# Attention and routed expert: a third buffer for transposed squares, no square or low part asked for at a chunk's last slot but one, and the last 64 keys' squares on ScalarE

## The chip, the cores and the metric

The kernel runs on one core of one Trainium2 chip. The metric is the time of one execution on the device, in microseconds. Three runs of the kernel before gave 2127.13, 2130.31 and 2130.52 us; the median is 2130.31 us.

## The reference

Eight batches go through squared-ReLU attention whose queries and keys are the same matrix `z`, then through an expert that works on the 128 best tokens of each batch. Cut to what matters:

```python
# B, S, D, d_qk = 8, 3136, 256, 64;  F = 1024;  capacity = 128
scores = (1 / S) * z @ z.transpose(0, 2, 1)          # symmetric
x = u * (np.maximum(scores, 0) ** 2 @ v)
out = x.copy()
for b in range(B):
    s = x[b] @ w_gate
    top = the 128 tokens with the largest s
    y = np.maximum(x[b, top] @ w1, 0) @ w2
    out[b, top] = x[b, top] + sigmoid(s[top])[:, None] * y
```

## The kernel before, in words

**Chunks and slots.** The 3136 queries of a batch are cut into seven chunks: c0 to c4 of 512 queries, c5 of 256 and c6 of 320. For each chunk the program goes through the keys in 13 slots, s0 to s12: twelve take a pair of key blocks (2 x 128 keys), and the last, the single slot, takes the 64 keys that are left. There are 8 x 7 x 13 = 728 slots in one sequence. In each, TensorE adds squares times `V` into four PSUM banks of the chunk (`acc`, L641; the pool has five banks). A square is split into a high part `hi` and a low part `lo` = square - hi, and both are multiplied. The products with `hi` come first, so `lo` may be ready a little later. At the end of a chunk the single slot is multiplied by `Vr` in place of `V`.

**New and old slots.** The scores are symmetric. A slot whose scores have not yet been worked out in this batch is new. TensorE multiplies them (`sc`, L510; for the single slot L494), ScalarE takes the ReLU (`a`, L514; single L500) and writes the square's high part (`hi`, L524; single L501). Then `a` is squared in place: for a pair by ScalarE (L530) or by VectorE (L534), as running sums of planned costs decide, and for the single slot by VectorE (L503). The low part is a subtraction, `lo`, on GpSimd or VectorE (both L614), as the same sums decide, and for the single slot on VectorE (L551). Squares that a later chunk needs are also transposed by VectorE into a staging tile `aT` (L577, L595 for the chunk's own block, L557 for the single slot), which SyncE stores to memory (L583, L589, L597, L565). An old slot fetches such squares back as `qk`, copies the high part (L474) and takes its low part. The tag `aT` has two buffers, so a transpose into it waits until the store of the tile two before has landed.

**What sets the order.** The program writes each engine's instructions out in an order of its own, slot by slot. In a slot, scores for three slots later are begun (`more_scores`), the products are issued (`mix`), and then a list of closing calls (`posts`) is run. Normally `settle_scores` stands in the middle of that list. It issues the outstanding squares, transposes and low parts of the slots ahead, which the function `low` writes, with the transpose ahead of the `lo`. `square_scores` issues the outstanding squares alone.

**A chunk's end.** At the single slot `finish` reads the four banks: ScalarE scales two of them (L722), and VectorE adds and multiplies, twice L735 and L736. Only then are banks free for the next chunk. In the slot before, s11, the list of closing calls is split. One call is made at once: `square_scores` in chunks c0 to c5 (not in the very first chunk), `settle_scores` otherwise. The rest is held for s12, where it comes behind L735 and L736. The code at L1653 is:

```python
if k + 2 < len(slots) and len(slots[k + 1][2]) == 1:

    now = square_scores if c <= WHOLE and (b or c) else settle_scores
    posts, held_posts = [now], [fn for fn in posts if fn is not settle_scores]
```

Between these calls the router's steps stand: gates and their sums (L943 to L967), the merge of the best tokens of the last batch's late chunks (L1201 to L1267) and the expert's products.

Of the kernel before, what the change touches and what calls it, by code (L numbers as in the profile page):

```python
# [88 lines left out]
def attention_then_routed_ffn(ctx: ExitStack, tc: tile.TileContext, zt, ut, v, wg, w1, w2, cst, cst16, keys, outs, at, cap):  # L89
# [388 lines left out]
    def scores(k):  # L478
# [9 lines left out]
        if n == 1:  # L488
# [12 lines left out]
            nc.scalar.activation(hi[:, 0, :w], a, AF.Square)  # L501
            spend(act=0.39 + 0.0024 * w)
            lows.append((k, a, hi[:, :, :w], (), lambda: nc.vector.tensor_tensor(a, a, a, op=ALU.mult)))  # L503
            return
# [37 lines left out]
    def low(k, a, hi, pieces, square):  # L542
# [5 lines left out]
        if n == 1:  # L548
            w = w // 2
            hi, lo = hi[:, 0], hi[:, 1]  # L550
            nc.vector.tensor_tensor(lo, a, hi.bitcast(F32), op=ALU.subtract)  # L551
            spend(dve=0.25 + 0.002 * w)

        def turned_single():
            x = w // 2
            t = work.tile([P, GT, 2, P], F32, name="aT", tag="aT", bufs=2).rearrange("p m q x -> p (m q x)")[:, :w]
            nc.vector.transpose(  # L557
# [9 lines left out]
        def turned():  # L567
# [3 lines left out]
            elif turns(k):  # L571
                t = work.tile([P, GT, 2, P], F32, name="aT", tag="aT", bufs=2)
                x = w // GT
# [17 lines left out]
            elif is_first(k):  # L591
                t = work.tile([P, GT, 2, P], F32, name="aT", tag="aT", bufs=2).rearrange("p m q x -> p (m q x)")[:, :CH]
                for q in range(2):
                    to = t.rearrange("p (m t q a) -> p q m t a", m=GT, t=2, q=2)[:, q]
                    nc.vector.transpose(to, a[:, q].rearrange("p (m t a) -> p m t a", t=GT, a=Q)[:, :, 2:])  # L595
                    spend(dve=0.08 + 0.0006 * w)
                stores.append(lambda: nc.sync.dma_start(own[b % 2][c].rearrange("p m x -> p (m x)"), t))  # L597
# [681 lines left out]
    def expert(b, st, n, r0=0):  # L1279
# [51 lines left out]
        def turned():  # L1331
            view = st["ps"][:, : NK * P].rearrange("p (k r) -> p k r", r=P)[:, :, :m]
            if merged(b):
                x = work.tile([P, 2, NK, P], F32R, name="xs", tag="aT", bufs=2)
            elif put_off(b) and b == B - 2:
# [262 lines left out]
    for k, (b, c, js, is_old) in enumerate(slots):  # L1598
# [45 lines left out]
        settle_turns()  # L1644
        if len(js) == 1 and c == WHOLE:
            low(*lows.pop(0))
        settle_stores()
# [5 lines left out]
        if k + 2 < len(slots) and len(slots[k + 1][2]) == 1:  # L1653

            now = square_scores if c <= WHOLE and (b or c) else settle_scores
            posts, held_posts = [now], [fn for fn in posts if fn is not settle_scores]
        if late and c >= NCH - late:
# [81 lines left out]
```

## Time and profile before

| what | value |
|---|---|
| median of three runs | 2130.31 us |
| the profiled execution | 2133.84 us, of which the span from first to last instruction is 2132.1 us |
| TensorE busy (PE) | 2037.6 us, 96% of the span |
| VectorE (DVE), ScalarE (ACT), GpSimd (POOL) busy | 72%, 69%, 62% |
| mean granted clock of TensorE | 0.985 of full speed |

TensorE (PE) is the engine to read first. PEld is its weight load, which runs beside the products. SPq is SyncE's queue of DMA issues. In a row of a timeline the first number is the start in us from the start of the span, the second the duration in us; a bracket at the end tells how long the engine had been idle and what ended that.

### The profile page before, as it was taken

To read this page: it belongs to the slowest core of one execution; us is meant where nothing else is said; L and a number is where in the kernel's file an instruction comes from. 1 tells how busy PE (TensorE), PEld (TensorE's weight loads), DVE (VectorE), ACT (ScalarE), POOL (GpSimd) and SP (SyncE) were. 2 spreads that over 40 slices of the span, in tenths; PEclk is the share of its full clock that TensorE was granted. 3 is DMA by queue.
4 is the path that set the end of the run, shared out by engine and by line. 5 is a ranking of instruction groups with operands and counts; after the bars stand their busy time and mean duration, and the time that the engine had idled before them with its cause. 6 is when DMAs were issued, how large, how long until landed. Compare 5 with 4: busy or idle time off the path is not lost.

```text
span 2132.1 us, 51160 instructions
## 1 busy us (share of the span) xinstructions
PE 2037.6 (96%) x19700; PEld 1756.1 (82%) x19700; DVE 1536.0 (72%) x2707; ACT 1462.7 (69%) x1965; POOL 1315.4 (62%) x718
## 2 busy tenths in 40 slices
PE   8999999999899999999989999899998999999997
PEld 5788978879688797888978889788887988778786
DVE  9766688756886568865788568875687766867665
ACT  7676687666776567865778657776587766777553
POOL 5765577735776367763678546775377654776452
PEclk9999999999999999999999999999999999999999
DMA  6788767896668966788657876678866777666842
GB/s 181 199 231 219 223 184 199 243 242 191 186 183 226 249 181 183 211 226 229 191 173 214 233 217 196 186 205 227 229 193 187 195 187 204 192 177 178 225 143 76
DMA packets 450868, 426.94 MB, mean 200 GB/s; under 512 B 136576, under 2 KB 377792, under 8 KB 447808
## 3 DMA queue, kind: packets, MB, share of 16 engines
q1 hardware_dynamic: 449488, 421.18, 70.0%
q8 instruction: 154, 2.52, 0.5%
q0 software_dynamic: 768, 2.10, 0.3%
q14 instruction: 90, 0.74, 0.1%
q10 hardware_dynamic: 368, 0.39, 0.1%
HBM read 248.94 MB, written 174.60 MB: 199 GB/s over the span
## 4 chain that ended last, share of the span: by engine, by line
PE 68%; DMA 7%; DVE 5%; ACT 4%; SPq 3%; issue 2%; POOL 1%; POOLq 0%; ACTq 0%; DVEq 0%
PE acc L641 58%; PE sc L510 7%; DMA qk<-squares 2%; DMA zst<-in_zt 2%; ACT a L514 1%; ACT hi L524 1%; DVE lo L614 1%; PE h L1358 1%; DMA squares_narrow<-aT 1%; DMA squares<-aT 1%; DVE a L534 1%; DVE aT L577 1%; PE y L1401 1%; DVE acc L735 1%; SPq L589 1%
## 5 line engine op out<-in xcount | busy, mean ns | idle before, releaser
L641 PE MATMUL acc<-hi,V 64*128 64x512 f32 (+2 forms) x10752 | 1270.5, 364 | 22.9 <-DVE ut L736 20.6
L641 PEld LDWEIGHTS acc<-hi,V 64*128 64x128 f32 x10752 | 1004.3, 186 | 158.6 <-issue 30.2
L614 POOL TENSOR_TENSOR lo<-a,hi 128x1024 fp32r<-128x1024 f32 (+1 forms) x280 | 634.2, 2267 | 462.0 <-ACT a L530 207.5
L641 PE MATMUL acc<-lo,V 64*128 64x512 f32 (+2 forms) x5376 | 716.4, 364 | 40.4 <-DVE lo L614 26.0
L641 PEld LDWEIGHTS acc<-lo,V 64*128 64x128 f32 x5376 | 520.1, 186 | 106.8 <-DVE lo L614 29.4
L514 ACT ACTIVATE a<-sc 128x1024 f32<-128x1024 f32 (+2 forms) x345 | 327.7, 950 | 268.7 <-PE sc L510 255.3
L577 DVE STREAM_TRANSPOSE aT<-a 128x512 f32<-128x512 f32 (+1 forms) x494 | 317.2, 681 | 213.9 <-ACT a L530 173.9
L474 ACT CAST hi<-qk 128x1024 fp32r<-128x1024 f32 (+2 forms) x327 | 278.9, 855 | 150.8 <-PE acc L641 110.8
L524 ACT ACTIVATE hi<-a 128x1024 fp32r<-128x1024 f32 (+2 forms) x345 | 339.8, 985 | 39.1 <-PE acc L641 17.9
L614 DVE TENSOR_TENSOR lo<-qk,hi 128x1024 fp32r<-128x1024 f32 (+2 forms) x215 | 298.5, 1399 | 60.5 <-ACT hi L474 47.2
L614 POOL TENSOR_TENSOR lo<-qk,hi 128x1024 fp32r<-128x1024 f32 (+2 forms) x112 | 220.8, 1979 | 137.9 <-ACT hi L474 122.1
L530 ACT ACTIVATE a<-a 128x1024 f32<-128x1024 f32 (+2 forms) x261 | 256.4, 982 | 7.5
L534 DVE TENSOR_TENSOR a<-a 128x1024 f32<-128x1024 f32 (+1 forms) x84 | 153.4, 1827 | 63.2 <-ACT hi L524 56.3
L126 POOL TENSOR_TENSOR V<-vst,V 128x512 fp32r<-128x512 f32 x92 | 161.5, 1764 | 17.8 <-ACT V L125 17.2
L754 POOL TENSOR_TENSOR ut<-x,w_run 128x1024 f32<-128x1024 f32 (+2 forms) x52 | 131.5, 2529 | 37.1 <-DVE x L745 36.8
L126 POOL TENSOR_TENSOR ZL<-zst,ZH 64x256 fp32r<-64x256 f32 x70 | 75.8, 1083 | 62.6 <-ACT ZH L125 53.4
L510 PE MATMUL sc<-Z,ZH 64*128 64x512 f32 x480 | 101.6, 390 | 10.1 <-ACT a L514 9.5
L614 DVE TENSOR_TENSOR lo<-a,hi 128x1024 fp32r<-128x1024 f32 (+2 forms) x65 | 83.8, 1289 | 24.4 <-ACT a L530 22.0
L510 PE MATMUL sc<-Z,ZL 64*128 64x512 f32 x480 | 99.5, 378 | 0.8 <-DVE ZL L126 0.8
L510 PE MATMUL sc<-Zl,ZH 64*128 64x512 f32 x480 | 98.7, 378 | 0.0
L735 DVE SCALAR_TENSOR_TENSOR acc<-acc,x 128x512 f32<-128x512 f32 (+2 forms) x112 | 70.0, 625 | 26.4 <-PE acc L641 26.2
L722 ACT ACTIVATE x<-acc 128x512 f32<-128x512 f32 (+2 forms) x112 | 54.5, 538 | 45.4 <-PE acc L641 44.5
(221 smaller groups left out, 1796.9 us busy)
## 6 DMA issues: line engine op xcount, KB each, us to landing
squares<-aT SPq DMA_DIRECT2D x160, 512.0 KB, 3.3
qk<-squares SPq DMA_DIRECT2D x320, 256.0 KB, 6.2
squares_narrow<-aT SPq DMA_DIRECT2D x320, 128.0 KB, 3.2
qk<-squares_narrow SPq DMA_DIRECT2D x80, 512.0 KB, 4.3
out<-x SPq DMA_DIRECT2D x162, 128.0 KB, 3.4
ut<-in_ut SPq DMA_DIRECT2D x40, 512.0 KB, 5.6
vst<-in_v SPq DMA_DIRECT2D x158, 128.0 KB, 2.9
zmv<-in_zt SPq DMA_DIRECT2D x78, 128.0 KB, 4.3
```

Of the source, the lines that this page charges most:

```text
L126: (lo_on or nc.vector.tensor_tensor)(lo, src, hi.bitcast(F32), op=ALU.subtract)
L474: nc.scalar.copy(by(hi), src)
L510: nc.tensor.matmul(ps[:, q, :w], stationary(high, js[0] // 2, q), mov[m][rows], start=i == 0, stop=i == 2)
L514: nc.scalar.activation(a, ps[:, :, :w], AF.Relu)
L524: nc.scalar.activation(pieces[0][0](hi), pieces[0][1], AF.Square)
L530: nc.scalar.activation(a, a, AF.Square)
L534: square = lambda: nc.vector.tensor_tensor(a, a, a, op=ALU.mult)
L577: nc.vector.transpose(to, a[:, q].rearrange("p (m t a) -> p m t a", m=GT, a=Q))
L614: on.tensor_tensor(view(lo), src, view(hi).bitcast(F32), op=ALU.subtract)
L641: nc.tensor.matmul(bank[g][h][:, cols[g]], V[b, j][rows, i, h], mov[rows], start=(b, c, g, h) not in opened, stop=len(js) == 1 and n == 2,)
L735: nc.vector.scalar_tensor_tensor(rest, rest, SCALE * SCALE, sums[h], op0=ALU.mult, op1=ALU.add)
L754: nc.gpsimd.tensor_tensor(wx, runs, consts["wg_run"].rearrange("p (o r) -> p o r", o=1).broadcast_to([P, NB, RUN]), op=ALU.mult,)
```

## The change

There are three edits. The tag `aT` gets three buffers. At s11 the list `posts` is emptied: no square and no low part is asked for there, and all is held for s12. The single slot's in-place square goes from VectorE (L503) to ScalarE (new line 502), right behind the `hi` square, and two planned costs are adjusted to it. For the chunk c5 the outstanding square is called before `low` at the end of its single slot, since it has not been asked for earlier.

```diff
             nc.scalar.activation(hi[:, 0, :w], a, AF.Square)
-            spend(act=0.39 + 0.0024 * w)
-            lows.append((k, a, hi[:, :, :w], (), lambda: nc.vector.tensor_tensor(a, a, a, op=ALU.mult)))
+            nc.scalar.activation(a, a, AF.Square)
+            spend(act=0.52 + 0.0032 * w)
+            lows.append((k, a, hi[:, :, :w], (), lambda: None))
             return
...
             nc.vector.tensor_tensor(lo, a, hi.bitcast(F32), op=ALU.subtract)
-            spend(dve=0.25 + 0.002 * w)
+            spend(dve=0.15 + 0.001 * w)
...
-            t = work.tile([P, GT, 2, P], F32, name="aT", tag="aT", bufs=2).rearrange("p m q x -> p (m q x)")[:, :w]
+            t = work.tile([P, GT, 2, P], F32, name="aT", tag="aT", bufs=3).rearrange("p m q x -> p (m q x)")[:, :w]
...
-                t = work.tile([P, GT, 2, P], F32, name="aT", tag="aT", bufs=2)
+                t = work.tile([P, GT, 2, P], F32, name="aT", tag="aT", bufs=3)
...
-                t = work.tile([P, GT, 2, P], F32, name="aT", tag="aT", bufs=2).rearrange("p m q x -> p (m q x)")[:, :CH]
+                t = work.tile([P, GT, 2, P], F32, name="aT", tag="aT", bufs=3).rearrange("p m q x -> p (m q x)")[:, :CH]
...
-                x = work.tile([P, 2, NK, P], F32R, name="xs", tag="aT", bufs=2)
+                x = work.tile([P, 2, NK, P], F32R, name="xs", tag="aT", bufs=3)
...
         if len(js) == 1 and c == WHOLE:
+            lows[0][-1]()
             low(*lows.pop(0))
...
         if k + 2 < len(slots) and len(slots[k + 1][2]) == 1:
 
-            now = square_scores if c <= WHOLE and (b or c) else settle_scores
-            posts, held_posts = [now], [fn for fn in posts if fn is not settle_scores]
+            posts, held_posts = [], [fn for fn in posts if fn is not settle_scores]
```

The program's lines behind the added ones are numbered one higher in the changed kernel (L735 becomes L736). What the change does to the order of an engine's instructions is shown at three places.

The first is VectorE at the end of chunk c0 in batch b2, where the next chunk's slot s0 is a new one with the chunk's own block. Before:

```order
L577 STREAM_TRANSPOSE aT<-a 128x4x128 x2
L503 TENSOR_TENSOR a<-a 128x256
L551 TENSOR_TENSOR hi<-a,hi 128x256
L557 STREAM_TRANSPOSE aT<-a 128x256
L595 STREAM_TRANSPOSE aT<-a 128x8x32 x2
L614 TENSOR_TENSOR lo<-a,hi 128x1024
L735 SCALAR_TENSOR_TENSOR acc<-acc,x 128x512
L736 TENSOR_TENSOR ut<-acc,ut 128x512
L735 SCALAR_TENSOR_TENSOR acc<-acc,x 128x512
L736 TENSOR_TENSOR ut<-acc,ut 128x512
```

And in the changed kernel, at the same place of the same engine:

```order
L578 STREAM_TRANSPOSE aT<-a 128x4x128 x2
L552 TENSOR_TENSOR hi<-a,hi 128x256
L558 STREAM_TRANSPOSE aT<-a 128x256
L596 STREAM_TRANSPOSE aT<-a 128x8x32 x2
L615 TENSOR_TENSOR lo<-a,hi 128x1024
L736 SCALAR_TENSOR_TENSOR acc<-acc,x 128x512
L737 TENSOR_TENSOR ut<-acc,ut 128x512
L736 SCALAR_TENSOR_TENSOR acc<-acc,x 128x512
L737 TENSOR_TENSOR ut<-acc,ut 128x512
```

Only the single slot's square is gone here; the transpose L595 (now L596) and the `lo` of s0 still stand ahead of the freeing of the banks.

The second is VectorE at the end of chunk c2 in batch b2, where L534 squares the scores of the next chunk's slot s1. Before:

```order
L614 TENSOR_TENSOR lo<-qk,hi 128x1024
L534 TENSOR_TENSOR a<-a 128x1024
L735 SCALAR_TENSOR_TENSOR acc<-acc,x 128x512
L736 TENSOR_TENSOR ut<-acc,ut 128x512
L735 SCALAR_TENSOR_TENSOR acc<-acc,x 128x512
L736 TENSOR_TENSOR ut<-acc,ut 128x512
L595 STREAM_TRANSPOSE aT<-a 128x8x32 x2
L577 STREAM_TRANSPOSE aT<-a 128x4x128 x2
```

In the changed kernel:

```order
L615 TENSOR_TENSOR lo<-qk,hi 128x1024
L736 SCALAR_TENSOR_TENSOR acc<-acc,x 128x512
L737 TENSOR_TENSOR ut<-acc,ut 128x512
L736 SCALAR_TENSOR_TENSOR acc<-acc,x 128x512
L737 TENSOR_TENSOR ut<-acc,ut 128x512
L535 TENSOR_TENSOR a<-a 128x1024
L596 STREAM_TRANSPOSE aT<-a 128x8x32 x2
L578 STREAM_TRANSPOSE aT<-a 128x4x128 x2
```

The square moved from ahead of the four operations that free the banks to behind them. It does the same at the end of c3; at the ends of c4 and c5 the order is as before.

The third is VectorE at the end of chunk c6 of the last batch, where the rows from L1201 to L1251 are the last merge of the best tokens. Before:

```order
L1201 TENSOR_SCALAR beats,cnt_o<-row,so 128x128
L1203 SCALAR_TENSOR_TENSOR beats,cnt_o<-row,so,c_sb 128x128
L735 SCALAR_TENSOR_TENSOR acc<-acc,x 128x320
L736 TENSOR_TENSOR ut<-acc,ut 128x320
L735 SCALAR_TENSOR_TENSOR acc<-acc,x 128x320
L736 TENSOR_TENSOR ut<-acc,ut 128x320
L1201 TENSOR_SCALAR beats,cnt_o<-row,so 128x256
L1201 TENSOR_SCALAR beats,cnt_n<-row,col 128x128
L1201 TENSOR_SCALAR beats,cnt_n<-row,col 128x256
L1203 SCALAR_TENSOR_TENSOR beats,cnt_n<-row,col,c_sb 128x128
```

In the changed kernel:

```order
L1204 SCALAR_TENSOR_TENSOR beats,cnt_n<-row,col,c_sb 128x128
L552 TENSOR_TENSOR hi<-a,hi 128x160
L1246 TENSOR_REDUCE rk_31029<-cnt_n 128x2
L1250 TENSOR_REDUCE rk_31029<-cnt_o 128x1
L1252 SCALAR_TENSOR_TENSOR oh_31158<-rk_31029,c_sb 128x384
L736 SCALAR_TENSOR_TENSOR acc<-acc,x 128x320
L737 TENSOR_TENSOR ut<-acc,ut 128x320
L736 SCALAR_TENSOR_TENSOR acc<-acc,x 128x320
L737 TENSOR_TENSOR ut<-acc,ut 128x320
```

The whole chain of this merge now stands ahead of the last L735 (now L736), where before all of it but two rows stood behind.

## Rows read from the trace of the kernel before

**Rows 1.** The page, busy time by engine over the whole span.
```profile
PE 2037.6 (96%) x19700; PEld 1756.1 (82%) x19700; DVE 1536.0 (72%) x2707; ACT 1462.7 (69%) x1965; POOL 1315.4 (62%) x718
```

**Rows 2.** All waits: engine and line, releaser: us in total, times, longest.
```profile
PE acc L641 <- DVE lo L614: 26.0, 7, 4.7
...
DVE aT L595 <- DMA squares_narrow<-aT: 23.2, 5, 4.9
...
PE acc L641 <- DVE ut L736: 20.6, 21, 3.4
```

**Rows 3.** Timeline of all engines, end of c0 in batch b2.
```profile
574.81 1.03 ACT L514 ACTIVATE a<-sc 128x1024 f32<-128x1024 f32 x1 [2.60 <-PE sc L510]
...
576.96 1.06 ACT L530 ACTIVATE a<-a 128x1024 f32<-128x1024 f32 x1
...
579.92 1.09 PE L641 MATMUL acc<-hi,V 64*128 64x512 f32 x8
...
581.70 0.77 DVE L595 STREAM_TRANSPOSE aT<-a 128x256 f32<-128x256 f32 x2 [4.56 <-DMA squares_narrow<-aT]
...
582.40 3.25 DVE L614 TENSOR_TENSOR lo<-a,hi 128x1024 fp32r<-128x1024 f32 x1
...
585.70 1.22 PE L641 MATMUL acc<-lo,V 64*128 64x512 f32 x4 [4.69 <-DVE lo L614]
```

**Rows 4.** Windows of the six chunks c1, batches b1 to b6; PEclk behind POOL.
```profile
585.57:628.31 42.74, 42.61 (x362) 38.21 (x364) 33.72 (x97) 32.00 (x38) 28.55 (x14) 0.93 0.60 178
...
sum 252.26, PE 251.48 PEld 220.10 DVE 210.16 ACT 192.96 POOL 176.31; mean PE 41.91 PEld 36.68 DVE 35.03 ACT 32.16 POOL 29.38
```

**Rows 5.** Windows again, the chunk c2 of batch b2.
```profile
628.31:668.87 40.56, 40.56 (x367) 33.07 (x365) 31.80 (x90) 31.20 (x38) 29.08 (x15) 1.00 0.80 208
```

**Rows 6.** Timeline of all engines, end of c2 in batch b2.
```profile
666.64 0.62 PE L641 MATMUL acc<-hi,Vr 64*128 64x256 f32 x6
...
667.73 1.23 DVE L534 TENSOR_TENSOR a<-a 128x1024 f32<-128x1024 f32 x1 [2.25 <-ACT hi L524]
...
668.87 0.69 DVE L735 SCALAR_TENSOR_TENSOR acc<-acc,x 128x512 f32<-128x512 f32 x1
...
670.44 1.15 PE L641 MATMUL acc<-hi,V 64*128 64x512 f32 x7 [0.87 <-DVE ut L736]
...
671.54 0.76 DVE L595 STREAM_TRANSPOSE aT<-a 128x256 f32<-128x256 f32 x2
...
673.52 1.24 PE L641 MATMUL acc<-lo,V 64*128 64x512 f32 x8
```

**Rows 7.** Timeline of all engines, end of c3 in batch b2.
```profile
710.52 0.69 DVE L735 SCALAR_TENSOR_TENSOR acc<-acc,x 128x512 f32<-128x512 f32 x1
710.68 2.40 POOL L614 TENSOR_TENSOR lo<-a,hi 128x1024 fp32r<-128x1024 f32 x1 [7.95 <-DVE a L534]
...
715.85 1.27 PE L641 MATMUL acc<-lo,V 64*128 64x512 f32 x8
```

**Rows 8.** Timeline of PE, end of c3 in batch b0.
```profile
192.79 2.04 PE L641 MATMUL acc<-hi,V 64*128 64x512 f32 x7 [3.39 <-DVE ut L736]
```

**Rows 9.** Timeline of PE, end of c3 in batch b6.
```profile
1747.43 1.16 PE L641 MATMUL acc<-hi,V 64*128 64x512 f32 x7 [2.00 <-DVE ut L736]
```

**Rows 10.** Timeline of all engines, end of c6 in the last batch.
```profile
2095.77 0.34 DVE L1201 TENSOR_SCALAR_CACHE_REDUCE beats<-row,so 128x128 bf16<-128x128 f32 x1 [3.71 <-ACT row L1215]
...
2101.79 0.22 PE L1267 MATMUL ids<-what,oh 128*128 128x5 bf16 x2 [5.17 <-DVE oh L1251]
```

**Rows 11.** Groups of instructions by line: busy us, mean ns, idle before.
```profile
L503 DVE TENSOR_TENSOR a<-a 128x256 f32<-128x256 f32 (+2 forms) x56 | 43.6, 779 | 23.2 <-ACT hi L501 23.0
...
L501 ACT ACTIVATE hi<-a 128x256 fp32r<-128x256 f32 (+2 forms) x56 | 21.9, 391 | 2.9
```

**Rows 12.** Timeline of all engines, middle of c0 in batch b2.
```profile
564.06 3.41 DVE L534 TENSOR_TENSOR a<-a 128x1024 f32<-128x1024 f32 x1
...
571.01 1.19 PE L641 MATMUL acc<-lo,V 64*128 64x512 f32 x8 [0.69 <-POOL lo L614]
```

## Prediction, on record before the result

> **What bounds the kernel now.** I read the busy times first. PE is busy for 2037.6 us of a span of 2132.1 us, 96% [rows 1], so the time is PE's work, plus its idle time of about 94 us, plus what its work takes longer at a lower clock. No change here takes work from PE, so only the last two can move. The list of waits comes second, because it says on whom PE waits. Two of its rows touch the change: 26.0 us in 7 waits on a low part that VectorE computes (`lo`, L614), and 20.6 us in 21 waits on the freeing of banks (`ut`, L736). A third is VectorE's own: 23.2 us in 5 waits of the transpose L595 for a store to land [rows 2]. Whether VectorE's longest wait, 4.9 us, and PE's, 4.7 us, are the same stall is settled third, in the timeline of one place.
>
> At the end of c0 in b2, PE finishes the eight `hi` products of the next chunk's s0 at 579.92 + 1.09 = 581.01 and then stands for 4.69 us until `lo` is there. VectorE writes that `lo` from 582.40, for 3.25 us, right behind L595, and L595 had waited 4.56 us for a store to `squares_narrow` to land. What L595 reads was ready long before, since L530 squared that tile on ScalarE by 576.96 + 1.06 = 578.02 [rows 3]. So the buffer, not the data, is what is late. The same stall stands in b1 to b6 (4.71, 4.69, 2.25, 4.68, 4.66 and 4.70 us, together 25.7 of the 26.0), and a seventh one of 0.34 us stands in b0.
>
> Each long stall has a second price. In the chunk that follows it the granted clock falls (0.93 in b2), and the six such chunks take 252.26 us together [rows 4], while c2 in b2, of the same shape, runs at 1.00 and takes 40.56 [rows 5]: 252.26 - 6 x 40.56 = 8.9 us. From the clock column instead, 42.74 x 0.07 = 3.0 us are lost in b2 against 42.74 - 40.56 = 2.2 by the lengths, so the sum may be a third larger, 12. A lower bound of 4 would hold if half of the difference were the routing steps that run in c1.
>
> **The change part by part.**
>
> *Third buffer.* With it L595 waits for L530 alone. It starts at 578.02, takes 0.77, and `lo` starts at 578.8. At the 1.23 us that L534, an operation of the same size, takes alone [rows 6], it ends at 580.0, an us before PE asks for it at 581.01. At the 3.25 us that the row shows [rows 3], it ends at 582.0 and PE waits 1.0 us. Gain: 26.0 us, at worst 26.0 - 6 x 1.0 = 20; and the clock's 8.9, between 4 and 12. I take **-26.0** and **-8.9**. The Trainium skill, "SBUF — State Buffer", section "SBUF: two separate sides", says that an operation of VectorE with two inputs in SBUF and one of GpSimd take a shared pair of ports as an exclusive lock, and the later one is fully blocked; the spread from 1.23 to 3.25 us would be that lock, and by it the gain would be nearer to 20 wherever GpSimd is busy then.
>
> *Posts held back, where they release banks earlier.* At the ends of c2 and c3 the square L534 leaves its place ahead of L735. At c2 in b2, PE closes the last bank at 666.64 + 0.62 = 667.26, but L735 starts only at 668.87, because L534 stands there from 667.73 to about 668.9 [rows 6]. After the change L735 starts at about 667.36, the banks are free 1.5 us earlier, and the 0.87 us wait goes. Such waits are 1.34 us in b0, 0.87 in each of b1 to b6, and 1.21 in b7.
>
> *And where they make the low part later.* The square then starts behind the four operations, at 667.36 + (671.54 - 668.87) = 670.03, ends at 671.26, and GpSimd's `lo` of s1, 2.40 us long [rows 7], is ready at 673.7. PE asked for it at 673.52 [rows 6]; without the 0.87 us wait, and without the slower products just behind it, it asks at about 672.4. A new wait of 1.3 us takes the place of 0.87 + 0.25. Net +0.2 us, for six batches **+1.5** with rounding; b0 and b7 come out even.
>
> At c3 in b2 no wait goes, since L735 was not late there. L735 to L736 run from 710.52 to about 713.2, the square to 714.4, `lo` to 716.85, and PE wants it at 715.85 [rows 7]: a new wait of 1.0 us, for b1 to b5 **+5.2**. In b0 and b6 the change does help: there the square delayed L735 so that PE waited 3.39 us [rows 8] and 2.00 us [rows 9]. In b0 I leave 0.6 us of the wait; behind it seven products took 2.04 us [rows 8], against 1.15 behind the short wait at c2 [rows 6], and that half clock goes as well, in part. I take **-3.1** and, with a little of the same, **-3.0**; b7, where 1.89 us were waited behind routing steps that still stand there, **-0.5**. At the end of c0 in b0, the first chunk, `settle_scores` no longer stands ahead of L735 and a wait of 1.37 us goes: **-1.5**. The eight waits of 0.50 us at c4 stay, since the order there is as before. These terms sum to -1.4, and I would not vouch for their sign: they are differences of waits of about 1 us, so between -6 and +5.
>
> *The last merge.* PE waits 5.17 us for `oh` at 2101.79, which VectorE begins behind L735 and L736, after 3.71 us of waiting for `row` [rows 10]. From 2095.77 to 2101.79 are 6.0 us, of which L735 and L736 stand some 2.2 (an estimate from their 2.7 us at 512 queries [rows 6], the smaller shape allowed for), so the chain itself takes 3.8. After the change PE's steps of this merge are asked for about a slot earlier, some 2 us here, and the chain runs in one piece ahead of L735. If `row` comes 2 us earlier, `oh` is ready at 2097.6, 4.2 us sooner; if `row` does not, at 2099.6, and the finish of the last chunk is then 3 us later. I take **-3.5**, between 0 and -4.5.
>
> *The single slot's square on ScalarE.* VectorE loses 56 operations of 779 ns on average, 43.6 us. ScalarE gains 56; the operation of the same shape next to it, the `hi` square L501, takes 391 ns, 21.9 us for 56 [rows 11]. It is hidden, because ScalarE stands 2.60 us idle behind the single slot, waiting for the next scores [rows 3]; with that cover gone it would cost up to 21.9 us. Only at the end of c6 is ScalarE late already; there I put 0.12 us seven times, **+0.8**. The Trainium skill, "ScalarE: Activation LUTs", section "Rules for kernel authors", speaks against this edit: multiplications belong on VectorE, up to about three times faster in bf16. Here the data are float32 and the row of ScalarE is half as long; by the page's factor each square would have lost 0.26 us, or 15 us in all, were it on the path.
>
> *VectorE against GpSimd in mid-chunk.* In c0 a square on VectorE takes 3.41 us beside GpSimd, against 1.23, and PE waits 0.69 us for a `lo` of GpSimd's [rows 12]. The order of such pairs shifts with the planner's sums; I put 0, with -5 to +7 us over six batches.
>
> Sum: -26.0 - 8.9 - 1.4 - 3.5 + 0.8 = -39.0. The profiled execution took 2133.84 us and should come to 2094.8; the median shown stands 3.5 lower, 2130.31, so I forecast **2091 us**. The likeliest case has its own range of 2082 to 2101, from the bounds above taken as partly independent.
>
> **The rivals.**
>
> *Something else holds the `lo` of c1's first slot.* For it speaks the 3.25 us at its place, and that a store behind it in SyncE's queue may now be late; against it, that its data are ready at 578.02. If 2 us of each of the six waits stay, with half of the clock's loss: 2091 + 12 + 4.5 = 2107.
>
> *New waits cost the clock.* The new waits at the ends of c2 and c3 are 1.0 to 1.3 us, and the clock may fall behind each of the eleven by what it lost at c1 (8.9 / 6 = 1.5 us): 2091 + 16 = 2107. Against it: behind the 0.87 us at c2 seven products took 1.15 us, not the 2.04 us of b0's long wait [rows 6, 8].
>
> *Held low parts are late at nearly every chunk end: slower.* The change holds them at 47 ends (8 x 6, less the first). My sum holds 6 x 1.3 + 5 x 1.0 = 13 us of new waits. If each of the 47 waited 1.4 us, 66 us, the rest of the gain is gone: 2091 + 66 - 13 = 2144. It decides from (39 + 13) / 47 = 1.1 us per end. Against it stands the order of VectorE, which at c0, c4 and c5 keeps the square and `lo` ahead of the freeing as before.
>
> *ScalarE becomes late.* If all added squares land on the path: 2091 + 22 = 2113. The 2.60 us of idle time speak against it.
>
> *The buffer is not what is waited for.* If L595 still ends when it does, only the small terms stay: 2130 - 4 = 2126, no change that can be told.
>
> **How the numbers follow.** Forecast 0.66, the first two rivals 0.10 and 0.09, ScalarE 0.05, no buffer effect 0.05, slower 0.05. What a measurement can tell here is about 0.2%, 4.3 us. The first four are faster; the fifth is split between faster and the same. So faster 0.92, same 0.03, slower 0.05. The range of 2077 to 2112 reaches past the first two rivals and takes in the bounds of the unknown terms; it leaves out the last three cases and some of the forecast's tail.
>
> **What would show it.** In the profile after: no wait of this transpose (now L596) for `squares_narrow`, and PE's wait for `lo` by VectorE from 26.0 to under 6 us; clock near 1.00 in c1; the waits for L737 down from 20.6 to about 5, with new waits for a `lo` of GpSimd at the ends of c2 and c3, 1.0 to 1.3 us each; the last merge's wait of 5.17 us shorter by 3; ScalarE busy 22 us more, and not more often waited for. Wrong would be: L596 waiting for something else, or new waits at the ends of c0, c1, c4 and c5.

## The result, and the profile after

The changed kernel takes 2101.92 us (median of four runs, 2098.54 to 2105.29), the kernel before beside it 2129.44 us: a ratio of 0.9872, 95% interval 0.9853 to 0.9891, so 27 us faster. Forecast were 2091 us and a range of 2077 to 2112. The profiled execution took 2098.54 us and is the fastest of the four; against the 2133.84 us of the one before it is 35.3 us shorter, where the sum of the prediction had 39.0.

The list of waits of the changed kernel (us in total, times, longest):

```profile
PE acc L642 <- POOL lo L615: 33.6, 37, 2.4
...
DVE aT L596 <- ACT a L531: 28.7, 12, 4.0
...
DVE ge L952 <- DMA gates<-scores_there: 24.0, 6, 5.1
...
PE acc L642 <- DVE ut L737: 4.8, 12, 0.5
...
PE acc L642 <- DVE lo L615: 0.3, 1, 0.3
```

Against [rows 2]: PE's waits for a low part of VectorE fell from 26.0 to 0.3 us and those for the freeing of banks from 20.6 to 4.8; those for a low part of GpSimd, 14.1 us in the list of before, are now 33.6. A row is new: VectorE waits 24.0 us in six waits for the gates. The end of c0 in b2, all engines:

```profile
569.76 1.06 ACT L531 ACTIVATE a<-a 128x1024 f32<-128x1024 f32 x1
...
570.85 0.77 DVE L596 STREAM_TRANSPOSE aT<-a 128x256 f32<-128x256 f32 x2 [4.05 <-ACT a L531]
...
571.54 1.18 DVE L615 TENSOR_TENSOR lo<-a,hi 128x1024 fp32r<-128x1024 f32 x1
...
573.31 0.62 PE L642 MATMUL acc<-lo,V 64*128 64x512 f32 x4
```

The transpose now waits for its data, the low part takes 1.18 us where it took 3.25 [rows 3], and PE comes to it without a gap. The windows of the chunks c1 of b1, b2 and b6, and the sum of all six (the clock stands behind the POOL column):

```profile
312.55:355.43 42.88, 40.82 (x366) 32.92 (x364) 36.83 (x94) 35.88 (x43) 33.79 (x17) 1.00 0.73 218
572.65:613.25 40.60, 40.60 (x370) 33.44 (x368) 34.24 (x96) 35.09 (x43) 30.92 (x15) 1.00 0.66 196
...
1597.00:1639.71 42.71, 40.97 (x370) 33.36 (x368) 35.12 (x96) 35.18 (x43) 30.90 (x15) 1.00 0.63 184
sum 253.96, PE 245.08 PEld 199.75 DVE 211.11 ACT 211.34 POOL 188.29; mean PE 40.85 PEld 33.29 DVE 35.19 ACT 35.22 POOL 31.38
```

The clock is 1.00 where it was 0.93 to 0.96 [rows 4], and yet the six chunks are not shorter but 1.7 us longer in sum. Only b2 has the length that was expected. The other five hold a new wait; the chain to it in c1 of b1, all engines:

```profile
319.03 0.62 DVE L952 TENSOR_SCALAR_CACHE_REDUCE ge<-gates,k_sb 128x392 bf16<-128x392 f32 x1 [3.72 <-DMA gates<-scores_there]
...
319.35 4.89 POOL L615 TENSOR_TENSOR lo<-a,hi 128x1024 fp32r<-128x1024 f32 x2
...
322.92 1.33 DVE L911 TENSOR_TENSOR base<-place,flip 32x1 int32<-32x1 int32 x1
...
325.18 1.30 DVE L578 STREAM_TRANSPOSE aT<-a 128x512 f32<-128x512 f32 x2
...
326.60 1.03 ACT L515 ACTIVATE a<-sc 128x1024 f32<-128x1024 f32 x1 [1.36 <-DVE aT L578]
...
331.66 2.40 POOL L755 TENSOR_TENSOR ut<-x,w_run 128x1024 f32<-128x1024 f32 x1 [3.88 <-DVE x L746]
...
334.01 2.37 POOL L615 TENSOR_TENSOR lo<-a,hi 128x1024 fp32r<-128x1024 f32 x1
...
336.43 1.21 PE L642 MATMUL acc<-lo,V 64*128 64x512 f32 x8 [1.67 <-POOL lo L615]
```

VectorE reaches L952 3.72 us before the gates have landed. What stands behind it in its order is late: the transpose L578, for which ScalarE's ReLU waits, and L746, for which GpSimd's product L755 waits, which in turn holds up the low part that PE waits for. In the kernel before, VectorE had stood 4.56 us at L595 in b2 [rows 3], and the gates had landed when it came to them (0.4 us of waiting for them in all six batches). The ends of c2 and c3 are what the prediction said. At c2 in b2, VectorE, GpSimd and PE:

```profile
655.01 1.22 DVE L535 TENSOR_TENSOR a<-a 128x1024 f32<-128x1024 f32 x1
...
656.31 2.38 POOL L615 TENSOR_TENSOR lo<-a,hi 128x1024 fp32r<-128x1024 f32 x1 [9.70 <-DVE a L535]
...
658.74 1.20 PE L642 MATMUL acc<-lo,V 64*128 64x512 f32 x8 [1.25 <-POOL lo L615]
```

And at c3 in b2, PE:

```profile
702.07 1.19 PE L642 MATMUL acc<-lo,V 64*128 64x512 f32 x8 [0.72 <-POOL lo L615]
```

The held square L535 now stands behind L737, and GpSimd's low part is 1.25 us late at c2 and 0.72 at c3; the wait of 0.87 us before it [rows 6] is gone. And in the last merge, PE:

```profile
2069.62 0.49 PE L1209 MATMUL old<-diag,c_sb 128*128 128x128 f32 x2 [2.66 <-ACT diag L1184]
```

The 5.17 us wait for `oh` [rows 10] is gone; 2.66 us for the next step of the same merge stand in its place.

### The profile page after: what moved, and what is told of

It reads as the page before. It is cut to its first block, busy times and chain, and to the rows that moved or that the text cites. A ratio compares the mean times of both kernels' runs of the same rounds, so it can differ in the third digit from the quotient of the medians.

```text
span 2096.7 us, 51099 instructions
## 1 busy us (share of the span) xinstructions
PE 2024.4 (97%) x19700; PEld 1682.5 (80%) x19700; DVE 1504.4 (72%) x2646; ACT 1487.4 (71%) x2028; POOL 1302.3 (62%) x716
## 4 chain that ended last, share of the span: by engine, by line
PE 54%; DMA 9%; issue 7%; POOL 7%; ACT 6%; DVE 6%; SPq 5%; POOLq 0%; ACTq 0%; DVEq 0%
PE acc L642 46%; POOL lo L615 5%; PE sc L511 5%; DMA zst<-in_zt 2%; DVE a L535 2%; ACT a L515 2%; ACT hi L525 2%; DMA squares_narrow<-aT 1%; DVE aT L578 1%; SPq L753 1%; DMA qk<-squares 1%; DMA ut<-in_ut 1%; PE y L1402 1%; SPq L446 1%; ACT a L531 1%
## 5 line engine op out<-in xcount | busy, mean ns | idle before, releaser
L642 PE MATMUL acc<-hi,V 64*128 64x512 f32 (+2 forms) x10752 | 1242.5, 362 | 6.8 <-DVE ut L737 4.8
L642 PEld LDWEIGHTS acc<-hi,V 64*128 64x128 f32 x10752 | 952.1, 185 | 171.2 <-issue 13.0
L642 PE MATMUL acc<-lo,V 64*128 64x512 f32 (+2 forms) x5376 | 694.9, 362 | 34.0 <-POOL lo L615 33.6
L642 PEld LDWEIGHTS acc<-lo,V 64*128 64x128 f32 x5376 | 486.1, 185 | 121.2 <-POOL lo L615 52.8
L578 DVE STREAM_TRANSPOSE aT<-a 128x512 f32<-128x512 f32 (+1 forms) x494 | 316.2, 680 | 167.7 <-ACT a L531 162.6
L615 DVE TENSOR_TENSOR lo<-qk,hi 128x1024 fp32r<-128x1024 f32 (+2 forms) x216 | 318.0, 1483 | 68.9 <-ACT hi L474 54.4
L531 ACT ACTIVATE a<-a 128x1024 f32<-128x1024 f32 (+2 forms) x268 | 263.4, 983 | 7.6
L535 DVE TENSOR_TENSOR a<-a 128x1024 f32<-128x1024 f32 (+1 forms) x77 | 135.2, 1756 | 43.6 <-ACT hi L525 38.1
L755 POOL TENSOR_TENSOR ut<-x,w_run 128x1024 f32<-128x1024 f32 (+2 forms) x52 | 130.3, 2506 | 54.6 <-DVE x L746 52.6
L126 POOL TENSOR_TENSOR V<-vst,V 128x512 fp32r<-128x512 f32 x92 | 147.4, 1612 | 23.7 <-ACT V L125 23.7
L736 DVE SCALAR_TENSOR_TENSOR acc<-acc,x 128x512 f32<-128x512 f32 (+2 forms) x112 | 70.0, 625 | 78.7 <-PE acc L642 78.7
L511 PE MATMUL sc<-Z,ZL 64*128 64x512 f32 x480 | 92.8, 372 | 0.8 <-DVE ZL L126 0.8
L615 DVE TENSOR_TENSOR lo<-a,hi 128x1024 fp32r<-128x1024 f32 (+2 forms) x65 | 75.7, 1165 | 16.7 <-ACT a L531 16.6
```

The lines of the kernel that those rows point to most:

```text
L126: (lo_on or nc.vector.tensor_tensor)(lo, src, hi.bitcast(F32), op=ALU.subtract)
L511: nc.tensor.matmul(ps[:, q, :w], stationary(high, js[0] // 2, q), mov[m][rows], start=i == 0, stop=i == 2)
L531: nc.scalar.activation(a, a, AF.Square)
L535: square = lambda: nc.vector.tensor_tensor(a, a, a, op=ALU.mult)
L615: on.tensor_tensor(view(lo), src, view(hi).bitcast(F32), op=ALU.subtract)
L642: nc.tensor.matmul(bank[g][h][:, cols[g]], V[b, j][rows, i, h], mov[rows], start=(b, c, g, h) not in opened, stop=len(js) == 1 and n == 2,)
```

## The experiments

My theory after the result: the third buffer is nearly the whole gain; what it fell short by is VectorE's new wait for the gates; the held posts exchange one wait for another. The rivals: the three edits need one another, or VectorE's load, which the square on ScalarE lightens, is what PE waited for. All medians:

| kernel | median, us | before beside it | ratio, 95% interval |
|---|---|---|---|
| buffer alone | 2106.55 | 2129.71 | 0.9898 (0.9875 to 0.9921) |
| held posts alone | 2135.25 | 2129.71 | 1.0026 (1.0007 to 1.0045) |
| ScalarE's square alone | 2125.94 | 2129.71 | 0.9986 (0.9970 to 1.0003) |
| buffer and ScalarE | 2100.18 | 2129.71 | 0.9859 (0.9835 to 0.9882) |
| the change with two buffers | 2128.53 | 2130.72 | 0.9992 (0.9974 to 1.0009) |
| the change, count one slot later | 2097.91 | 2128.05 | 0.9856 (0.9826 to 0.9886) |
| the change, 16 squares on ScalarE | 2079.69 | 2128.05 | 0.9770 (0.9742 to 0.9799) |
| both of these | 2084.14 | 2128.05 | 0.9791 (0.9760 to 0.9821) |
| both, without the held posts | 2083.72 | 2128.05 | 0.9795 (0.9766 to 0.9825) |
| both, a slot given back | 2082.68 | 2130.72 | 0.9776 (0.9752 to 0.9801) |
| 16 squares, gates fetched first | 2075.91 | 2130.72 | 0.9754 (0.9728 to 0.9779) |
| the same, scores stored first | 2072.69 | 2126.25 | 0.9748 (0.9726 to 0.9770) |

To see where the time goes, I take from each trace the stretches between the first bank-freeing operation (L735, or L736 where lines are shifted) of one chunk and the next, and sum the eight stretches that end at the finish of the same chunk; the tail is what follows the last. The difference of these sums to the kernel before, in us (held posts free banks earlier at every end, so c0 and c6 are to be read together):

| kernel | c0 + c6 | c1 | c2 | c3 | c4 | c5 | tail |
|---|---|---|---|---|---|---|---|
| the change | -35.6 | +3.0 | -10.3 | +5.6 | +5.5 | +2.1 | -5.6 |
| buffer alone | -33.1 | +3.3 | +4.3 | +0.6 | -1.3 | -1.5 | 0.0 |
| buffer and ScalarE | -34.1 | +2.5 | +2.3 | -0.6 | -1.4 | +1.3 | -3.9 |
| count later | -35.2 | -9.2 | -14.8 | -5.4 | +10.7 | +21.6 | -5.2 |
| 16 squares | -35.5 | +4.9 | -10.6 | -4.6 | -4.8 | +0.3 | -4.0 |
| both | -36.8 | -9.3 | -14.5 | -15.2 | +4.3 | +25.0 | -3.5 |
| both, slot back | -34.9 | -9.3 | +3.8 | -2.7 | -4.8 | +0.6 | -2.8 |

**The buffer alone.** The only edit to the kernel before, in all four places:

```diff
-name="aT", tag="aT", bufs=2)
+name="aT", tag="aT", bufs=3)
```

> The kernel before with a third aT buffer and nothing else; the order of every engine is that of before. Theory (the buffer is nearly the whole gain): the 25.7 us of waits for the low part of c1's first slot go, and 9 to 13 us of slower clock behind them; VectorE, no longer stalled there, reaches the gates before they have landed and waits for them as in the changed kernel, which gives back 1.7 us of waiting on PE in five of eight batches, 8 us in all. The 20.6 us of waits for the freeing of banks stay. Sum: 2129 - 26 - 11 + 8 = 2100 us, between 2095 and 2106. Rival (the three edits need one another: with the square and the single slot's square still ahead of L735, something else is late at the end of c0): waits of 2 us or more stay there in b1 to b6, 2110 to 2122 us.

It gave 2106.55 us, 23 us less than before; the theory's bounds ended at 2106, the rival's began at 2110. Its list of waits:

```profile
PE acc L641 <- POOL lo L614: 24.0, 30, 2.4
...
DVE ge L951 <- DMA gates<-scores_there: 20.9, 6, 4.1
...
PE acc L641 <- DVE ut L736: 19.7, 21, 2.0
...
PE acc L641 <- DVE lo L614: 0.3, 1, 0.3
```

The 26.0 us are gone by this edit alone, and the wait for the gates comes with it. The waits of some 1.66 us in c1 stand in all six batches here.

The buffer also took away a wait that the prediction's sum left out. In the list of before:

```profile
DVE aT L577 <- DMA squares<-aT: 31.5, 13, 5.5
...
1852.17 1.31 DVE L577 STREAM_TRANSPOSE aT<-a 128x512 f32<-128x512 f32 x2 [1.64 <-DMA squares<-aT]
```

The transposes L577 waited for the same two buffers; with three, none of this wait is left. In c0 of b7 it had reached PE: L577 (second line, of VectorE's timeline) stood 1.64 us and again 0.56 us ahead of a count (L897) that PE waited 2.39 us for, and the clock of that chunk was 0.93. With the buffer alone PE waits there for the count by 1.14 and 1.01 us, the clock is 1.00, and the stretch is 3.0 us shorter.

**The held posts alone.**

```diff
-            now = square_scores if c <= WHOLE and (b or c) else settle_scores
-            posts, held_posts = [now], [fn for fn in posts if fn is not settle_scores]
+            posts, held_posts = [], [fn for fn in posts if fn is not settle_scores]
```

For c5 the outstanding square is called behind its single slot, as in the change.

> The kernel before with nothing asked for at s11, two aT buffers and the single slot's square on VectorE. Theory: the stalls of 4.7 us at the end of c0 stay. Waits for the freeing of banks fall from 20.6 to about 5 us, and new waits for GpSimd's low part at the ends of c2 and c3, 1.2 and 0.7 us, take their place; with the clock behind the long waits of b0 and b6 and the last merge the edit is worth 2 to 6 us: 2123 to 2128 us. Rival (the held posts are a main part of the gain): 2115 us or less.

2135.25 us, slower by 0.07 to 0.45%: outside of both expectations. PE's waits for `ut` fell to 4.7 us as expected, those for GpSimd's low part rose to 27.0, and 22.9 us for VectorE's stayed. Its profiled execution, 2131.65 us, lies 2.2 us under the profiled one of before, so this trace does not show where the 5.5 us of the medians are.

**ScalarE's square alone.**

```diff
-            spend(act=0.39 + 0.0024 * w)
-            lows.append((k, a, hi[:, :, :w], (), lambda: nc.vector.tensor_tensor(a, a, a, op=ALU.mult)))
+            nc.scalar.activation(a, a, AF.Square)
+            spend(act=0.52 + 0.0032 * w)
+            lows.append((k, a, hi[:, :, :w], (), lambda: None))
...
-            spend(dve=0.25 + 0.002 * w)
+            spend(dve=0.15 + 0.001 * w)
```

> The kernel before with the single slot's in-place square on ScalarE and its planned costs, two aT buffers, s11 as before. Theory: the stall at the end of c0 stays, since it is a store that is waited for and not VectorE's time; ScalarE is late by about 0.35 us early in c0 of seven batches: 2129 to 2134 us. Rival (43.6 us taken from VectorE pay, since VectorE's lateness is what PE waits for): 2120 us or less.

2125.94 us: 4 us less, at the edge of what can be told (the interval reaches to 1.0003), and better than the theory had it, though far from the rival. The stall stays, as the theory says (PE waits 26.1 us for VectorE's low part). What I had not expected is the tail: it is 3.9 us shorter, since the planner, told that VectorE has less to do, asks for the last merge a slot earlier. The wait in it, PE:

```profile
2093.16 0.49 PE L1209 MATMUL old<-diag,c_sb 128*128 128x128 f32 x2 [2.65 <-ACT diag L1184]
```

**Buffer and ScalarE, without the held posts.** The two edits together.

> The changed kernel with s11 as before, so without the held posts. Theory: as with the buffer alone, plus 2 us for ScalarE: 2097 to 2108 us, and within 5 us of the changed kernel's 2102, since the held posts exchange one wait for another. Rival (the held posts are needed to gain from the buffer): 2112 us or more.

2100.18 us, as the theory has it, with an interval (0.9835 to 0.9882) that overlaps that of the whole change (0.9853 to 0.9891). The held posts add nothing that can be measured.

**The change with two buffers.** The changed kernel with `bufs=2` again.

> The changed kernel with two aT buffers; the order of every engine is that of the changed kernel. Theory (the buffer is what removes the stall at the end of c0): the stalls of 4 to 5 us stay in most of b1 to b6, with the clock behind them; the held posts and the square on ScalarE give together 2 to 6 us: 2122 to 2132 us. Rival (the stall at the end of c0 depends on when the stores are issued, which the held posts have moved): 2115 us or less.

2128.53 us, no change to before, as the theory says. Its waits:

```profile
DVE aT L596 <- DMA squares_narrow<-aT: 40.6, 7, 8.8
...
PE acc L642 <- DVE lo L615: 24.8, 9, 7.0
...
DVE ge L952 <- DMA gates<-scores_there: 0.8, 3, 0.4
```

With the stall back, VectorE's wait for the gates is covered again: 0.8 us where the changed kernel has 24.0. Without the buffer the other two edits are worth nothing that can be measured; the buffer does not need them.

**The count one slot later.**

```diff
-            tasks = [([fold], set_out, 2), ([], bring_back, 1)]
+            tasks = [([fold], set_out, 2), ([], bring_back, 2)]
```

> The changed kernel with one slot more between the fetch of the gates (L944) and the first count on them (L952). Theory (in the changed kernel VectorE reaches L952 before the gates have landed and stands 3.1 to 5.1 us; all that is queued behind it is late, down to the low part that PE waits 1.67 us for in c1 of five batches and the 2.06 us in c2 of b1): VectorE's waits for the gates fall from 24.0 to under 5 us, these waits of PE go, and the clock behind them; c1 is shorter by some 2 us in five batches: 2086 to 2096 us. Rival (the wait in c1 comes from GpSimd's own load, the product L755 ahead of the low part): the 1.67 us stay, 2099 to 2104 us.

2097.91 us, above the theory's range and below the rival's. The waits in c1 are gone, as it says: the six chunks c1 of b1 to b6 take 40.28 us in five and 40.57 in one, 242.0 us in sum. But VectorE still waits 14.7 us for the gates, and every later step of the router and the expert moved by a slot too; in c5 a new wait of 2.9 us and slow clock stand, and c5 is 19.5 us longer in sum than in the changed kernel. The planner's sums moved with it: among others, one low part of c1 in each of the six batches (of `vst`, 128x512) went from GpSimd to VectorE. It stands behind the place of the 1.67 us wait, so it does not explain that the wait is gone, but it can have a share in c1's length.

**The squares of s1 at c3 and c4 on ScalarE.** 16 squares change the engine; nothing else moves.

```diff
-        if busy["act"] < busy["dve"] + 1.0 + dve + (0.16 + 0.00236 * w if turns(k) else 0.0):
+        if k % SLOTS == 1 and 2 < c < WHOLE or busy["act"] < busy["dve"] + 1.0 + dve + (...):
```

> The changed kernel with the square of slot s1 of the chunks c3 and c4 on ScalarE in all batches: 16 squares change the engine and nothing else moves. Theory (the held square, behind L737, is what makes the low part late): the waits for GpSimd's low part at the ends of c2 and c3, 1.24 us eight times and 0.72 us in five or six batches, go, some 13 us in all with the clock: 2085 to 2096 us. Rival (ScalarE has no room there: its copies of the high parts, L474, come 1 us later, and PE waits for these in place of the low part): no more than 4 us faster, 2097 to 2104 us.

2079.69 us, 22 us under the change and more than expected. PE's waits for GpSimd's low part fell from 33.6 to 19.1 us. At the end of c2 in b2:

```profile
648.20 0.70 DVE L736 SCALAR_TENSOR_TENSOR acc<-acc,x 128x512 f32<-128x512 f32 x1 [2.41 <-PE acc L642]
...
648.57 1.06 ACT L531 ACTIVATE a<-a 128x1024 f32<-128x1024 f32 x1
...
649.71 2.42 POOL L615 TENSOR_TENSOR lo<-a,hi 128x1024 fp32r<-128x1024 f32 x1 [7.24 <-ACT a L531]
```

The square runs on ScalarE beside L736, and GpSimd starts its low part 1.5 us after L736 begins, not some 4. So the held square was what made it late. I had priced eight waits of 1.24 and six of 0.72 us; b7's 2.29 us at the end of c3 and smaller ones in b0 and b6 went as well, some 17 us in all at these two places; by the stretches c3 and c4 are 20.5 us shorter than in the changed kernel.

**Both.**

> Both edits, the count one slot later and the 16 squares on ScalarE. Theory: the two waits are independent, and the gains add, some 11 and 13 us: 2071 to 2086 us. Rival (they share a wait, or ScalarE becomes late): no better than the better of the two, 2086 us or more.

2084.14 us: the gains do not add. By the stretches c1 to c3 are 28.7 us shorter than with the 16 squares alone, and c4 and c5 are 33.8 us longer. A wait in c5 stands for what is lost. At the end of c4 in b2, PE:

```profile
733.56 1.22 PE L642 MATMUL acc<-lo,V 64*128 64x256 f32 x8 [2.92 <-POOL lo L615]
```

And GpSimd at the same place:

```profile
731.16 1.02 POOL L1412 DMA_INDIRECT out<-y,ids  x1 [17.07 <-PE acc L642]
732.25 2.49 POOL L615 TENSOR_TENSOR lo<-qk,hi 128x512 fp32r<-128x512 f32 x2
```

The expert's last step, the scatter of its rows (L1412), now stands in GpSimd's order ahead of the low parts of c5, and PE waits 2.92 us for the first.

**Both, without the held posts.** As above, with s11 as in the kernel before.

> The same with s11 as in the kernel before, so without the held posts: third buffer, single slot on ScalarE, count one slot later, 16 squares on ScalarE. Theory (the held posts only move a square from ahead of the freeing of the banks to behind it; with the square on ScalarE they have nothing left to do at c2 and c3): within 5 us of the kernel with both edits and held posts, 2074 to 2088 us. Rival (the held posts are worth 10 us or more of themselves, at the other chunk ends): 2088 us or more.

2083.72 against 2084.14 us. With the square on ScalarE, too, the held posts are worth nothing that can be measured.

**Both, with the slot given back behind the last count.**

```diff
-            tasks.append(([], [lambda: settle_shares(last), lambda: (masks(), run_up())], 2, False))
+            tasks.append(([], [lambda: settle_shares(last), lambda: (masks(), run_up())], 1, False))
```

> The kernel with the 16 squares on ScalarE, the first count on the gates one slot later, and one slot less of rest behind the last count, so that the expert's steps stand where they stood: the order of PE and of SyncE's queue is that of the kernel with the 16 squares, and only VectorE's counting moves. Theory (what the later count lost by itself was the expert's last step at the end of c4, pushed to where GpSimd's low part is needed): the 2.9 us waits in c5 do not come, VectorE's waits for the gates fall from 21.9 to 15 us or less, the 1.6 us waits in c1 go: 2062 to 2073 us. Rival (the chain of counts has no slot to spare, and PE waits for its end, the totals in c2, by 2 us in six batches instead of one): 2075 to 2083 us.

2082.68 us: here the rival was right. (The low part of `vst` in c1 moved to VectorE here, too, which the expectation had not foreseen.) c5 is as it was, c1 is 9.3 us shorter than before, but at the end of the chain PE waits:

```profile
DVE ge L952 <- DMA gates<-scores_there: 15.1, 6, 2.7
...
PE ahead L1039 <- DVE upto L1032: 13.1, 6, 2.8
```

**The gates fetched first.** The changed kernel with the 16 squares, and in SyncE's order L944 ahead of the four stores L566.

```diff
-        settle_stores()
+        tasks = [(ops, post() if getattr(post, "__name__", "") == "bring_back" else post) for ops, post in tasks]; settle_stores()
```

> The kernel with the 16 squares on ScalarE, where SyncE issues the fetch of the gates (L944) ahead of the four stores of the single slot's squares (L566) instead of behind them; the order of all other engines is the same. Theory (the gates are late because their eight issues stand behind these stores in SyncE's queue): the gates land some 3 us earlier, VectorE's waits for them fall from 21.9 to under 6 us, the 1.6 us waits of PE in c1 go, with the clock behind them: 2060 to 2072 us. Rival (the fetch has to wait for the scores' own store to land, and what is late is that round trip): SyncE waits there, the stores behind it are late, 2076 to 2085 us.

2075.91 us: between theory and rival, and with an interval that overlaps that of the 16 squares alone. The waits in c1 went in b1 and b2 and stayed in b3 to b6. SyncE and VectorE at the end of c0 in b4:

```profile
1063.64 0.34 SPq L935 DMA_DIRECT2D scores_there<-G  x1
...
1070.04 4.36 SPq L944 DMA_DIRECT2D gates<-scores_there  x8
...
1076.20 0.62 DVE L952 TENSOR_SCALAR_CACHE_REDUCE ge<-gates,k_sb 128x392 bf16<-128x392 f32 x1 [4.06 <-DMA squares_narrow<-aT]
```

From the store of the scores to the start of the fetch are 6.4 us, in whose second half SyncE issues nothing. VectorE still waits 4.06 us here, and 19.4 in all. The bracket names a store, L566, whose issue now follows the fetch on a semaphore that they share; what L952 reads are the gates, and in this batch the last of their eight transfers landed at 1075.79. The queue was only a part of the reason. The order of VectorE, ScalarE and GpSimd is that of the 16 squares alone, so the two waits that went in c1 went with the earlier landing, while GpSimd's load was the same.

**The scores stored first.** In addition L935 ahead of the four fetches L446.

> The kernel with the 16 squares on ScalarE and the gates fetched ahead of the single slot's stores, where the store of the scores that the gates are fetched from (L935) is also issued ahead of the four fetches of squares (L446) before it, as soon as VectorE has written them; otherwise only a cast of ScalarE's (Vr, L125) moves by three places. Theory (the gates' landing is set by the round trip that begins with this store, since SyncE stood some 3 us before the fetch with its store outstanding): the store starts some 1.5 us earlier and the gates land as much earlier; VectorE's waits at L952 fall from 19 to under 13 us, and the 1.65 us waits of PE that are left in c1 of b3 to b6 go: 2063 to 2073 us, a ratio of 0.969 to 0.973. Rival (the fetched squares are now late, or the fetch of the gates itself is what takes long beside other transfers): 2074 to 2082 us.

2072.69 us, but a ratio of 0.9748, not the 0.969 to 0.973 expected: it cannot be told from the kernel without it. VectorE's waits for the gates are 17.1 us. The waits in c1 stand in b2, b3 and b5 and not in b1, b4 and b6.

## Why the prediction was right, point by point

**The wait of L595.** Right, in place and size: 26.0 us forecast, all but 0.3 gone, and shown by the buffer alone and by the change with two buffers. Of the two bounds for the low part's duration the lower one held, 1.18 us, and the lock that the prediction named did not come into play: GpSimd is idle at that moment in all six batches, and the low part takes 1.18 or 1.19 us in each. Before, in b2, GpSimd stood in the way:

```profile
582.22 2.34 POOL L614 TENSOR_TENSOR lo<-a,hi 128x1024 fp32r<-128x1024 f32 x1 [5.71 <-ACT a L530]
```

VectorE's low part began 0.18 us behind it and took 3.25 us [rows 3], to 1.1 us past its end; in b3, where VectorE's began first, it took 1.18.

**The clock behind it.** The clock came back to 1.00, but the term "-8.9" failed as time: I took c1 as c2's length with nothing else late. The six chunks should have come to 252.26 - 8.9 = 243.4 us and came to 253.96. With the count later they take 242.0, so the term itself was about right, and a wait of VectorE's that the old stall had covered costs some 10 to 12 us in c1 (the lower figure against six times the 40.60 us of b2, which has no such wait). My first rival had the kind of thing (a part of the gain is kept back), but a wrong place, the low part of s0; the gates' landing I had not priced.

**The held posts.** -1.4 us forecast. For c2 to c4 the terms were +1.5 + 5.2 - 3.1 - 3.0 - 0.5 = +0.1, and the stretches give -10.3 + 5.6 + 5.5 = +0.8. The new waits were 1.25 and 0.72 us, where I had 1.3 and 1.0. In the medians, too, the edit is worth nothing. In b2 to b5 the stretches c2 and c3 together changed by -0.4 to +0.2 us, and c4 by +1.0: the rival of 1.5 us of clock lost behind each such wait fell, and so did the one of low parts late at nearly every end.

**The last merge.** -3.5 forecast, -5.6 in the tail. That 3.9 us of it came from the edit to ScalarE's square and its planned costs, only the single edits showed; with the held posts alone the tail is 0.5 us longer, and the other 1.7 us come only with the two together.

**The square on ScalarE.** +0.8 forecast. By the stretches, buffer and ScalarE against the buffer alone are 5.9 us better, 3.9 of these in the tail, and 6 in the medians. The price that I had looked for did not show: PE's waits for ScalarE's `a` are 10.1 us with buffer and ScalarE, 9.5 before; the 12.0 of the whole change, short waits early in c0, come with the held posts, since the held posts alone have them too (12.2). On the rule of the Trainium skill for this edit ("ScalarE: Activation LUTs", section "Rules for kernel authors"): the runs do not bear out a loss here. The square takes 392 ns on ScalarE (L502, mean of 56), where it took 779 on VectorE [rows 11].

**The sum.** By the stretches, c0, c1 and c6 came to -32.6 us, where the terms are -26.0 - 8.9 - 1.5 + 0.8 = -35.6; c2 to c4 to +0.8 against +0.1; c5 to +2.1 against nothing; the tail to -5.6 against -3.5. Together 3.7 us short. That the sum is so near is partly luck, since two misses of opposite sign offset each other. c1 came to +3.0 where -8.9 was forecast, 11.9 us too long. c0 and c6 came to -35.6 where the terms are -26.0 - 1.5 + 0.8 = -26.7, 8.9 us more: around the ends of c0 in b1 to b6 the changed kernel is 30.7 us shorter, where 25.7 had been waited for, in b0 4.0 where 1.5 were forecast, and at the last c6 1.0. (In b7 the 3.0 us of the buffer alone are not there in the changed kernel: PE waits 2.06 us for a count in that c0, at a clock of 0.97.) What the 5 us beyond the waits in b1 to b6 consist of is not shown. The median of 2101.92 us lies inside the outer range, but 0.9 us above the likeliest case's own, and nearer to the 2107 of the first two rivals than to the forecast of 2091. The rest of the 11 us between the forecast and the median is that the profiled execution of the changed kernel is the fastest of its runs, and the one of before lay above its median.

## What to carry to other kernels

When a stall is taken away, list every wait that ended during it on all engines: each is now exposed, and its followers must be walked through to the engine that bounds the kernel. An operation on which two engines wait in turn, as the held square here, is better moved to a third engine that is idle at that moment than shifted behind one of the two. A step of a long chain that is moved by a slot moves the whole chain; look at where its last step lands.

## What the runs showed of the hardware that was not expected

The wait in c1 goes with what happens to an operation with 32 elements. In the changed kernel L911 on VectorE took 1.33 us in c1 of b1, above. There it ended at 324.25, and GpSimd's two low parts, begun at 319.35, ended at 324.24. In b2, VectorE and GpSimd:

```profile
582.37 0.15 DVE L911 TENSOR_TENSOR base<-place,flip 32x1 int32<-32x1 int32 x1
582.51 2.40 POOL L615 TENSOR_TENSOR lo<-a,hi 128x1024 fp32r<-128x1024 f32 x1 [0.35 <-POOL lo L615]
```

Here it fell between two operations of GpSimd and took 0.15 us, and b2 alone has no wait in c1. The operation before it and the four behind it, which read one tensor each (the four take a scalar per partition besides), keep their times. In the kernel with the scores stored first it took 2.26, 1.83 and 2.08 us in the three batches with the wait, and 0.59, 0.26 and 0.26 in the other three. Over the changed kernel and the three with the 16 squares and the count unmoved, 24 chunks, one has the wait with a short L911 (b5 of the changed kernel, after 5.14 us of waiting for the gates).

That one is no exception if L911's end is looked at and not its length. Take the six kernels that have three buffers and the count unmoved (these four, buffer alone, and buffer and ScalarE): in 35 of their 36 chunks L911 ends 0.01 us past the end of a low part of GpSimd's, and only in b2 of the changed kernel does it fall between two. VectorE's wait for the gates and the time of L911 together are 5.0 to 5.4 us in the 30 chunks with the wait of some 1.65 us, and 2.5 to 3.2 us in the six without; nothing lies between. So waits for the gates of anything from 2.7 to 5.1 us end in nearly the same delay, because L911 comes out only at the end of a low part, and these ends lie some 2.4 us apart. That is what the Trainium skill, "SBUF — State Buffer", section "SBUF: two separate sides", says of an operation of VectorE with two inputs in SBUF: GpSimd's, begun first, blocks it to its end. The link from L911 to the wait is read from the traces and was not tried by itself. What makes the gates' round trip as long as it is stays open.
